# Experts without loops: two nested tests an expert, one test at the end for long lists, w_out four pieces ahead

## The chip, the cores and the metric

One core of one Trainium2 chip runs the whole kernel as one program. The metric is the device time of one execution in microseconds (us), and for the kernel before it is the median of three runs.

## The reference

Three stages follow each other, in fp32:

```
x   = attention(q_l, k_l, v_l, q_g, k_g, v_g)  # 4 x 8 heads, 512 local + 32 global tokens; local: window of 32 keys and the globals
e   = argmax(x @ w_gate)                       # x: 2176 tokens x 512; 8 experts, one per token
y   = gate_w * sigmoid(x @ w_output_gate)[e] * (relu(x @ w1[e]) @ w2[e])   # w1[e]: 512 x 1024, w2[e]: 1024 x 512
h   = y @ w_in;  g = (a0 + a1 h + a2 h^2 + a3 h^3) / (1 + |b0||h| + |b1| h^2 + 1e-6)
out = g @ w_out                                # w_in: 512 x 2048, w_out: 2048 x 512
```

The inputs give the eight experts 422, 331, 253, 249, 220, 149, 434 and 118 tokens. Which parts of the program run depends on these numbers, since the kernel tests them on the chip.

## The kernel before, in words

**Precision.** Every fp32 operand of the two MoE stages is split into a high and a low part (`hi`, `lo`, type fp32r), and each product is three matmuls: hi by hi, hi by lo, lo by hi. ScalarE (ACT) makes `hi` by a cast, and VectorE (DVE) or GpSimd (POOL) makes `lo` by a subtraction. The weights of an expert are 16 pieces of 128x512 in `slot[e % 2]`; while expert e computes, the pieces of expert e+1 are loaded into four `raw` buffers and split into the other slot (`split_set`, lines 697 to 701).

**Experts.** `wide(e)` (L884) computes the first 256 tokens of expert e (296 of expert 0): eight steps of 12 matmuls into `ph` (L898), a relu into `hT` (ACT L903, DVE L904), and, two steps later, 12 matmuls into `acc` (L910). At its end `acc` is copied to the tile `yt` (L916) and stored to `ybuf` (L839), and 512 entries of the expert's token list go from `idxT` to `toks` (L917); both stores are issued by ACT. A background generator (`todo`, L927) runs beside the matmuls by a plan: `s` splits a weight piece, `g` gathers a block of 128 tokens from `xbuf` (POOL, an indirect DMA into one of four `xg` buffers, L782), `x` scales it (ACT L794), `p` transposes it on TensorE (L807) and splits it (ACT L787, DVE L788). So the tokens of expert e+1 are prepared during expert e: three blocks, 384 tokens.

**Tokens beyond 256.** `single(e, j, x)` (L845) computes one block of 128 tokens. `beyond(e)` (L992) runs it behind a test on the chip, `cnt[e] > 256`; inside, a test `cnt[e] > 384` leads to `more` (L966), a loop of the hardware (`tc.For_i`, L968) over the blocks from the fourth on. An iteration transposes the block that was gathered before (L971), fetches the next one, runs `single` and stores 128 entries of the list column-wise to `toks` (L973). `beyond(e)` is called inside `wide(e + 1)`, behind its first step. For expert 0, one `single` behind a test (L1030) and a loop `more(0, j0, end0)` stand between `wide(0)` and `wide(1)`; with these inputs the loop has no iteration. Then block 2 of expert 1 is scaled and transposed (L1033, L1034), and `wide(1)` begins. With these inputs the test at L993 is true for experts 1 and 6, and the loop runs once, for expert 6.

**Conversion.** `w_in` and `w_out` come as 64-bit floats, and DVE makes fp32 of a piece by three integer operations (L718, L721, L724). `conv_step` (L735) does it for all 16 pieces of `w_in` and two of `w_out` (`NPRE = 2`) during experts 1 to 6, three pieces an expert, `c` in the plan. Two pieces `r64` are loaded ahead; the result stands in one tile `f32` (`NF = 1`) until SyncE's queue (SP) has stored it to `wf` in HBM (L742), from where it is loaded later like a weight.

**The second MoE stage.** `moe2` goes through 80 steps, five chunks of tokens by 16 columns of `w_in`. A step has 12 matmuls into `ph` (`gemm1`, L1111), the rational function on ACT, POOL and DVE (`elem`, L1114 to L1147), and matmuls of an earlier step into `acc` (`gemm2`, L1159). In the first 16 steps a generator `w_out` (L1179) brings one piece of `w_out` a step: a piece that was converted before is only split (L1193, L1194), any other is first converted on DVE by the same three operations. `columns` (L1213) turns the token list once, by a transpose into `acc3` and a copy by ACT to `order` (L1216), after step 2.

**What sets the order.** The order on every engine is the order in which the program issues: there is no planner. Engines wait for each other by semaphores. Before `moe2`, a test `off[7] < 512` (L1057) guards a reload of the first chunk, which expert 7's stage prepares ahead (`early`, L1041); it is false here.

Of the kernel before, what the change touches and what calls it, by code (L numbers as in the profile page):

```python
# [7 lines left out]
F32 = mybir.dt.float32  # L8
# [38 lines left out]
def plan(n, **at):  # L47

    o = [""] * n
    for t in "scxpg":  # L50
        for k in at.get(t, ()):
            o[k] += t
    return o


NPRE, NCONV = 2, 9

LOADS = [l for j in range(NPRE // 2) for l in ((4 * j, 4 * j + 2), (4 * j + 1,), (4 * j + 3,))]
# [13 lines left out]
STE = lambda nc, ch, i: nc.vector.tensor_copy if ch == 0 else nc.scalar.copy  # L72
LEAD = 2
WB = 1
NF = 1
YQ = lambda nc: nc.scalar
AQ = lambda nc: nc.gpsimd
AFTER = 1
# [25 lines left out]
class Build:  # L104
# [540 lines left out]
    def lists(self):  # L645

        self.nc.vector.tensor_tensor(out=self.wrap, in0=self.tab, in1=self.wrap, op=ALU.subtract)
        yield
        yield
        pt = self.ps_m.tile([128, 512], F32, tag="xps", name="lgT")[:, 0:128]  # L650
        self.nc.tensor.transpose(pt, self.wrap[:, 0:128], self.ident)
        yield
        self.nc.scalar.copy(self.idxT, pt)

    def ahead(self):

# [69 lines left out]

    def conv_init(self, pool):
        self.r64 = [pool.tile([128, 512], I64, name=f"r64_{n}") for n in range(2)]
        self.f32 = [pool.tile([128, 512], I32, name=f"f32_{n}") for n in range(NF)]

    def conv_first(self):
        for q in range(2):
# [2 lines left out]
    def conv_step(self, k):  # L735

        q, n = divmod(k, 3)
        if not 0 <= q < 16 + NPRE:
            return
        self.conv_op(self.r64[q % 2], self.f32[q % NF], n)  # L740
        if n == 2:
            CQ(self.nc).dma_start(out=self.wf[q], in_=self.f32[q % NF].bitcast(F32))  # L742
            if q + 2 < 16 + NPRE:
                n = q + 2 if q < 14 else 16 + 2 * (q - 14)
                CQ(self.nc).dma_start(out=self.r64[q % 2], in_=self.t["w64"][n])

    def counts(self):
# [15 lines left out]
        nc.vector.tensor_scalar(out=o[:, 2:3], in0=o[:, 2:3], scalar1=7, scalar2=None, op0=ALU.logical_shift_right)  # L763
        nc.vector.tensor_tensor(out=o[:, 2:3], in0=o[:, 2:3], in1=o[:, 3:4], op=ALU.mult)


    def expert_tiles(self, pool):
        mp, cp = self.mp, self.cp
        self.xs = pool.tile([128, 2, 4, FIRST], F32R, name="xs")
        self.xgs = [mp.tile([128, DM + 1], F32, name=f"xg{n}") for n in range(2)]  # L770
        for x in self.xgs:
            self.nc.gpsimd.memset(x, 0.0)
        ix = mp.tile([128, 5], I32, name="ix")
        self.idx0, self.ixo = ix[:, 0:3], ix[:, 3:5]
        self.cnt_i = cp.tile([1, 2, E], I32, name="cnt_i")
        self.cnt_f = cp.tile([1, 4, E], F32, name="cnt_f")
        c = cp.tile([1, 5], I32, name="cnt_x")
        self.cnt0, self.cnt_x = c[:, 0:1], c[:, 1:5]

    def gather(self, j, ix, n=NT, rows=128):  # L780

# [30 lines left out]
    def experts(self, st, first, gate):  # L812
# [29 lines left out]

            AQ(nc).dma_start(out=self.ybuf[:, :, FIRST:FIRST + 128], in_=y)

        def single(e, j, x, at=0, put=None):  # L845

            W = self.slot[e % 2]
# [36 lines left out]
        def wide(e, j, n, x, bg, last=True, acc=None, before=None):  # L884
# [29 lines left out]
            def end():  # L914
                for m in range(4):
                    (nc.scalar.copy, nc.vector.tensor_copy)[m % 2](yt[:, m, :n], acc[m][:, :n])  # L916
                YQ(nc).dma_start(out=self.toks[bass.ds(off[e], MOST), :].rearrange("(j p) o -> j (p o)", p=128),  # L917
                                 in_=self.idxT[NBLK * e:NBLK * e + MOST // 128])
                store(e, j, n, yt[:, :, :n], YQ(nc))

            if last:
# [36 lines left out]
        blocks = lambda e, bs=range(3): [(e, b) for b in bs if e < E]  # L958

        def fetch(e, i):  # L960

            ixo = self.ixo[:, 0:1]
            nc.gpsimd.tensor_copy(ixo, self.idx[:, bass.ds(i + NBLK * e, 1)])
            self.gather(NX - 1, ixo)

        def more(e, j, end):  # L966

# [18 lines left out]
        def expert(e, early=lambda: ()):  # L986

            plan = PLANW if e < E - 1 else PLANW7
            wide(e, 0, BASE, X(e), weave(todo(e, plan, None, blocks(e + 1), blocks(e, (3,)) + blocks(e + 1, (2,)) + blocks(e + 2, (0, 1))),
                                         iter(early())), before=(lambda: beyond(e - 1)) if e > 1 else None)  # L990

        def beyond(e):  # L992
            with tc.If(cnt[e] > BASE):  # L993
                single(e, 2, X(e), 256)
                with tc.If(cnt[e] > BASE + 128):
                    more(e, 3, (cnt[e] + 127) // 128)

        def woven():

            g, sp = self.gate(B - 1, woven=GW), todo(0, "s" * 8, 0)  # L1000
            for n in count():
                for _ in range(GS):
# [11 lines left out]
            yield from weave(todo(0, PLAN0, 1, blocks(1, (0, 1)) + blocks(0, (2, 3)),  # L1014
                                  blocks(1, (0, 1)) + blocks(0, (2, 3)) + blocks(2, (0, 1)) + blocks(1, (2,))),
                             self.lists())


# [2 lines left out]
        gate.close()  # L1021
        pools.append(PP("ps_t2", 1))
        self.conv_init(P("cv"))
        vals = nc.values_load_multi_w_load_instructions(self.cnt_i.rearrange("a b e -> a (b e)"), min_val=0, max_val=NT)[1]
        cnt, off[:] = vals[:E], vals[E:]
        more0, j0, end0 = nc.values_load_multi_w_load_instructions(self.cnt_x[:, 0:3], min_val=0, max_val=NBLK)[1]
# [14 lines left out]
        def early():  # L1041
            def steps():
                for _ in range(EL):
                    yield
                y0 = [x[:, :DM].rearrange("p (m t) -> p m t", m=4) for x in self.xgs[:3] + hr[:1]]
# [32 lines left out]
    def moe2(self):  # L1078
        nc, tc, out = self.nc, self.tc, self.t["out"]
        with ExitStack() as st:  # L1080
# [142 lines left out]
            for s in range(n + SK):  # L1223
# [104 lines left out]
```

## Time and profile before

| | us |
|---|---|
| median of three runs | 895.53 (894.07 to 903.0) |
| the profiled execution: time, span | 894.73, 892.8 |
| PE busy (share of the span) | 807.1 (90%) |
| DVE busy | 639.9 (72%) |
| ACT busy | 538.9 (60%) |
| POOL busy | 366.5 (41%) |

The page says where each engine is busy over the whole span. Three stretches have different limits: attention and routing up to about 190 us, the experts from there to 457 us, and `moe2` to the end. A busy share is an average over these, so the stretches are read one by one: the timeline (instructions in order of time, with the idle time of the engine before each and what ended it) and the table of windows (busy time of each engine in a stretch, with the granted TensorE clock).

### The profile page before, as it was taken

How to read it: one execution, taken by the hardware profiler on the slowest of the kernel's cores; microseconds unless marked ns; L12 is line 12 of the kernel's file. 1: busy time of each engine (PE TensorE's matmuls, PEld its weight loads, DVE VectorE, ACT ScalarE, POOL GpSimd, SP SyncE). 2: the span in 40 equal slices, each digit the busy share in tenths (PEclk: the TensorE clock that was granted, in tenths of full speed). 3: DMA queues.
4: the chain of work that ended last, by engine and by line, in shares of the span. 5: the costliest groups of instructions: out<-in, count | busy, mean ns of one | idle time of the engine just before them, and what ended most of it. 6: DMA issues, size and time to landing. Idle time of an engine off the chain costs nothing. (4 is left out here: it accounts for less than half of the span.)

```text
span 892.8 us, 17092 instructions
## 1 busy us (share of the span) xinstructions
PE 807.1 (90%) x6069; PEld 675.5 (76%) x6069; DVE 639.9 (72%) x1436; ACT 538.9 (60%) x1211; POOL 366.5 (41%) x409
## 2 busy tenths in 40 slices
PE   7999998986998999996778888789999999999994
PEld 4766765875988999974766666578887888988882
DVE  4778777752656887741349999997886888688684
ACT  3667666443554566631346655557777777778774
POOL 3445546452434666521434333443233323332422
PEclk9999999998998999998799999989999999999998
DMA  8798872581838799830431321200100000000000
GB/s 287 254 326 264 272 251 78 155 253 37 282 112 277 251 317 323 277 130 24 122 117 43 124 66 63 72 30 29 36 1 36 24 0 25 24 1 1 36 0 36
DMA packets 50512, 112.90 MB, mean 126 GB/s; under 512 B 9104, under 2 KB 22593, under 8 KB 48362
## 3 DMA queue, kind: packets, MB, share of 16 engines
q1 hardware_dynamic: 41642, 97.18, 34.1%
q0 software_dynamic: 4480, 10.14, 3.4%
q10 hardware_dynamic: 4288, 4.29, 1.4%
q8 instruction: 55, 0.90, 0.4%
q14 instruction: 47, 0.39, 0.1%
HBM read 96.99 MB, written 18.98 MB: 130 GB/s over the span
## 5 line engine op out<-in xcount | busy, mean ns | idle before, releaser
L1159 PE MATMUL acc<-slot,gh 128*128 128x512 f32 x544 | 174.6, 401 | 12.0 <-ACT gh L1132 3.3
L1123 POOL TENSOR_TENSOR q<-q,ab 128x384 f32<-128x384 f32 (+1 forms) x80 | 105.8, 1322 | 188.3 <-ACT q L1122 183.5
L1111 PE MATMUL ph<-x2c,slot 128*128 128x512 f32 (+1 forms) x576 | 136.1, 387 | 14.8 <-DVE u L1125 9.9
L701 POOL TENSOR_TENSOR slot<-raw,slot 128x512 fp32r<-128x512 f32 x80 | 109.0, 1366 | 94.8 <-ACT slot L697 89.5
L1111 PEld LDWEIGHTS ph<-x2c,slot 128*128 128x128 f32 x576 | 108.8, 194 | 38.0 <-DVE u L1125 13.0
L1159 PEld LDWEIGHTS acc<-slot,gh 128*128 128x128 f32 x544 | 102.3, 190 | 36.7 <-ACT gh L1132 4.6
L1159 PE MATMUL acc<-slot,gl 128*128 128x512 f32 x272 | 108.9, 400 | 0.5 <-DVE gl L1133 0.5
L910 PE MATMUL acc<-hT,slot 128*128 128x256 f32 (+1 forms) x768 | 104.9, 287 | 3.1 <-DVE hT L904 3.1
L910 PEld LDWEIGHTS acc<-hT,slot 128*128 128x128 f32 x768 | 97.9, 191 | 3.3 <-DVE hT L904 3.3
L697 ACT CAST slot<-raw 128x512 fp32r<-128x512 f32 x144 | 84.4, 618 | 14.1 <-DVE yt L916 5.2
L1132 ACT CAST gh<-u 128x384 fp32r<-128x384 f32 (+1 forms) x80 | 44.6, 557 | 77.2 <-DVE u L1147 76.4
L1140 DVE SCALAR_TENSOR_TENSOR q<-q,r 128x384 f32<-128x384 f32 (+1 forms) x80 | 50.0, 625 | 54.6 <-ACT r L1136 54.4
L1111 PE MATMUL ph<-xa,slot 128*128 128x384 f32 x384 | 74.6, 343 | 7.4 <-DVE u L1125 7.4
L1111 PEld LDWEIGHTS ph<-xa,slot 128*128 128x128 f32 x384 | 68.5, 191 | 13.2 <-DVE u L1125 11.0
L1135 ACT ACTIVATE r<-q,cab 128x384 f32<-128x384 f32 (+1 forms) x80 | 52.7, 659 | 42.3 <-POOL q L1123 42.3
L701 DVE TENSOR_TENSOR slot<-raw,slot 128x512 fp32r<-128x512 f32 x64 | 64.2, 1006 | 14.4 <-ACT slot L697 13.3
L317 POOL TENSOR_SCALAR pr<-ex,r 128x128 f32<-128x128 f32 x128 | 46.9, 379 | 65.2 <-PE sc L263 20.8
L898 PE MATMUL ph<-xa,slot 128*128 128x256 f32 x384 | 56.0, 302 | 12.1 <-issue 11.0
L898 PEld LDWEIGHTS ph<-xa,slot 128*128 128x128 f32 x384 | 52.7, 209 | 12.9 <-issue 11.2
L1159 PEld LDWEIGHTS acc<-slot,gl 128*128 128x128 f32 x272 | 51.7, 190 | 14.2 <-DVE gl L1133 2.1
L1122 ACT ACTIVATE q<-ab,cab 128x384 f32<-128x384 f32 (+1 forms) x80 | 59.8, 748 | 0.0
L299 ACT ACTIVATE ex<-sm,mx 128x128 f32<-128x128 f32 x128 | 50.3, 395 | 15.7 <-POOL pr L317 7.5
(207 smaller groups left out, 1529.5 us busy)
## 6 DMA issues: line engine op xcount, KB each, us to landing
raw<-in_w_dram SPq DMA_DIRECT2D x78, 512.0 KB
vw<-in_vw_dram SPq DMA_DIRECT2D x16, 1024.0 KB
r<-in_w_dram SPq DMA_DIRECT2D x18, 512.0 KB
kw<-in_kw_dram SPq DMA_DIRECT2D x16, 384.0 KB
wf<-f SPq DMA_DIRECT2D x18, 256.0 KB
raw<-wf SPq DMA_DIRECT2D x9, 512.0 KB
qt<-in_qT_dram SPq DMA_DIRECT2D x32, 128.0 KB
xbuf<-xrow SPq DMA_DIRECT2D x8, 512.0 KB
```

The lines of the kernel that those rows point to most:

```text
L299: nc.scalar.activation(ex[:, h], src[:, h], AF.Exp, bias=mx[:, h:h + 1], scale=-1.0, accum_out=ssum[:, h:h + 1])
L317: nc.gpsimd.tensor_scalar(out=pr[:, h], in0=ex[:, h], scalar1=r[:, h:h + 1], scalar2=1.0, op0=ALU.mult, op1=ALU.mult)
L697: nc.scalar.copy(hi, r)
L701: eng.tensor_tensor(out=lo[:, c], in0=r[:, c], in1=hi[:, c].bitcast(F32), op=ALU.subtract)
L898: nc.tensor.matmul(ph, lhsT=W[:, b, 2 * k + s // 4, c:c + 128], rhs=x[:, a, k, :n], start=(i == 0), stop=(i == 11))
L910: nc.tensor.matmul(acc[m][:, :n], lhsT=W[:, b, 8 + f, 128 * m:128 * m + 128], rhs=hT[f % nh][:, a, :n], start=(f == 0 and i == 0), stop=(f ...
L1111: nc.tensor.matmul(ph[:, :w], lhsT=l[a], rhs=r[b], start=(k == 0 and i == 0), stop=(k == 3 and i == 2))
L1122: nc.scalar.activation(q, ab, AF.Identity, scale=b1, bias=b0)
L1123: nc.gpsimd.tensor_tensor(out=q, in0=q, in1=ab, op=ALU.mult)
L1135: nc.scalar.activation(r0, q, AF.Ln, bias=eps1)
L1140: nc.vector.scalar_tensor_tensor(out=q, in0=q, scalar=1.0 + 1e-6, in1=r0, op0=ALU.add, op1=ALU.mult)
L1159: nc.tensor.matmul(accs[i], lhsT=l[a], rhs=Wo[:, b, f, :], start=(f == 0 and j == 0), stop=(f == 15 and j == 2))
```

## The change

1. `more` is no longer called for experts 1 to 7. The inner test leads to one more `single(e, 3, ...)`, whose block is prepared like the others: four blocks per expert are scaled and transposed during the expert before instead of three. The plans get one more `x` and `p` (and other places for `g`). Block 3 of expert 1 is gathered during expert 0 and scaled and transposed with block 2 between `wide(0)` and `wide(1)`.
2. Expert 0's loop stands behind a test (`again0 > 0`).
3. What lies beyond 512 tokens of any expert stands behind one test, `rare > 0`, at the end, where `off[7] < 512` stood. Behind it an expert's weights are loaded and split once more, and a loop runs over the rest of its list. `rare` is worked out with the other counts (three DVE operations) and loaded with them: five registers instead of three.
4. Each expert stores its whole list (up to 18 rows of 128) instead of four rows; the column-wise store of the loop is gone.
5. `NPRE = 4`: four pieces of `w_out` (0, 2, 4, 6) are converted ahead, the last two during expert 7. A second conversion buffer is taken from the tile `yt`, for the middle one of an expert's three pieces.
6. `columns` runs after step 1 instead of 2; the four blocks of the first chunk are loaded into the four `xg` buffers instead of three of them and `hr0`; the dead gather of expert 7's stage is gone.

```diff
-NPRE, NCONV = 2, 9
+NPRE, NCONV = 4, 9
-PLANW = plan(32, s=range(0, 31, 2), c=(2, 3, 4, 12, 13, 14, 22, 23, 24), g=(1, 6, 18, 24), x=(1, 2, 14), p=(5, 8, 19))
-PLANW7 = plan(32, s=range(2, 18, 2), g=(1,))
+PLANW = plan(32, s=range(0, 31, 2), c=(2, 3, 4, 12, 13, 14, 22, 23, 24), g=(1, 3, 18, 24), x=(1, 2, 14, 16), p=(5, 8, 19, 22))
+PLANW7 = plan(32, s=range(2, 18, 2), c=(4, 5, 6, 16, 17, 18))
-PLAN0 = plan(16, s=range(1, 9), g=(0, 0, 1, 2, 11, 12, 14), x=(6, 7, 9, 10), p=(7, 8, 11, 13))
+PLAN0 = plan(16, s=range(1, 9), g=(0, 0, 1, 2, 11, 12, 14, 15), x=(6, 7, 9, 10), p=(7, 8, 11, 13))
...
-        self.conv_op(self.r64[q % 2], self.f32[q % NF], n)
+        self.conv_op(self.r64[q % 2], self.f32[q % 3 % 2], n)
...
+        f = o[:, 4:5]
+        nc.vector.tensor_reduce(out=f, in_=self.cnt_i[:, 0], axis=AX.X, op=ALU.max)
+        nc.vector.tensor_scalar(out=f, in0=f, scalar1=MOST, scalar2=None, op0=ALU.is_gt)
+        nc.vector.scalar_tensor_tensor(out=f, in0=self.cnt_i[:, 1, E - 1:E], scalar=128 * CH[0], in1=f, op0=ALU.is_lt, op1=ALU.max)
...
                 with tc.If(cnt[e] > BASE + 128):
-                    more(e, 3, (cnt[e] + 127) // 128)
+                    single(e, 3, X(e), 384)
...
+        def reload(e):
+            w = yt.rearrange("p m t -> p (m t)")[:, 0:1024]
+            for pc in range(8):
+                ...
+                AQ(nc).dma_start(out=w, in_=src)
+                for q in range(2):
+                    hi, lo = (self.slot[1][:, i, 2 * pc + q, :] for i in range(2))
+                    nc.scalar.copy(hi, w[:, 512 * q:512 * q + 512])
+                    nc.vector.tensor_tensor(out=lo, in0=w[:, 512 * q:512 * q + 512], in1=hi.bitcast(F32), op=ALU.subtract)
+        def rest(e):
+            reload(e)
+            with tc.For_i(1, (cnt[e] + 127) // 128 - MOST // 128 + 1, 1) as k:
+                ...
+                single(e, None, self.xa, put=..., W=self.slot[1])
...
-        fetch(0, j0)
         with tc.If(more0 > 0):
             single(0, 2, self.xs, put=store_rest)
-        more(0, j0, end0)
-        self.scale(2, 128, S1)
-        self.prep(2, self.xa, ps_t(), 256, scale=False)
+        with tc.If(again0 > 0):
+            fetch(0, j0)
+            more(0, j0, end0)
+        for b in (2, 3):
+            self.scale(b, 128, S1)
+            self.prep(b, self.xa, ps_t(), 128 * b, scale=False)
...
         beyond(E - 1)
-        with tc.If(off[E - 1] < 128 * CH[0]):
+        with tc.If(rare > 0):
+            ...
+            for e in range(E):
+                with tc.If(cnt[e] > MOST):
+                    rest(e)
             for n in range(CH[0]):
-                self.load_y(n, nc.scalar)
+                self.load_y(n, AQ(nc))
                 self.x2_prep(n, self.x2c, n)
...
-                if s == 2:
+                if s == 1:
                     columns()
```

## Rows read from the trace of the kernel before

**Rows 1.** Timeline, expert 0's end: start, duration us, engine, line, [idle before <-releaser]

```profile
206.90 0.90 PE L880 MATMUL pt<-ident,hr 128*128 128x128 f32 x4 [0.52 <-ACT hr L876]
...
213.48 0.72 ACT L794 ACTIVATE xg<-xg 128x512 f32<-128x512 f32 x1 [5.00 <-issue]
...
214.26 1.11 PE L807 MATMUL pt<-ident,xg 128*128 128x128 f32 x4 [6.46 <-ACT xg L794]
...
215.02 6.09 PE L898 MATMUL ph<-xa,slot 128*128 128x256 f32 x36
215.41 0.59 ACT L787 CAST xa<-pt 128x512 fp32r<-128x512 f32 x1 [1.21 <-PE pt L807]
```

**Rows 2.** The loop's line L968: sequencer instructions, ns min/median/max, first to last start us

```profile
L968 ACTq EVENT_SEMAPHORE  x12: 38/38/2142, 210.0 to 213.2; - x12
...
L968 SPq EVENT_SEMAPHORE  x10: 27/28/562, 426.9 to 428.0; - x10
```

**Rows 3.** Timeline, expert 6's first single block, and the loop's last store

```profile
386.03 4.28 PE L865 MATMUL ph<-slot,x2c 128*128 128x512 f32 x18
...
398.69 0.90 PE L880 MATMUL pt<-ident,hr 128*128 128x128 f32 x4 [0.52 <-ACT hr L876]
...
419.43 0.57 POOL L973 DMA_DIRECT2D toks<-ix  x1
```

**Rows 4.** Timeline, wide(7) going on behind expert 6's loop

```profile
428.66 5.28 PE L898 MATMUL ph<-xa,slot 128*128 128x256 f32 x24 [10.99 <-issue]
...
433.77 1.58 PE L910 MATMUL acc<-hT,slot 128*128 128x256 f32 x12
```

**Rows 5.** Timeline, wide(2) going on behind expert 1's single block

```profile
256.48 3.00 PE L898 MATMUL ph<-x2c,slot 128*128 128x256 f32 x24 [0.78 <-ACTq L995]
```

**Rows 6.** Windows, wide(2) and wide(3): us, busy PE PEld DVE ACT POOL, PEclk, DMA, GB/s

```profile
256.50:286.60 30.10, 26.50 (x205) 25.99 (x205) 22.59 (x30) 15.79 (x32) 16.64 (x13) 0.89 0.67 226
286.60:311.70 25.10, 24.34 (x204) 24.14 (x204) 19.15 (x30) 15.62 (x32) 16.07 (x12) 1.00 0.80 256
```

**Rows 7.** Timeline, the end of wide(2)

```profile
272.61 0.33 SPq L742 DMA_DIRECT2D wf<-f  x1
...
277.68 2.18 DVE L718 TENSOR_SCALAR f<-r 128x512 int32<-128x512 int32 x1 [2.37 <-issue]
...
280.98 2.50 PE L910 MATMUL acc<-hT,slot 128*128 128x256 f32 x10 [3.09 <-DVE hT L904]
```

**Rows 8.** Timeline, a block's four transposes inside wide(4)

```profile
340.62 0.46 PEld L807 LDWEIGHTS pt<-ident,xg 128*128 128x128 f32 x4
```

**Rows 9.** Windows, steps 4 to 15 of moe2

```profile
489.40:580.00 90.60, 72.52 (x293) 55.36 (x292) 90.17 (x110) 51.91 (x85) 37.52 (x23) 0.96 0.27 82
```

**Rows 10.** Timeline of DVE, one operation of elem in three steps of moe2

```profile
481.34 0.68 DVE L1140 SCALAR_TENSOR_TENSOR q<-q,r 128x512 f32<-128x512 f32 x1
...
487.46 0.69 DVE L1140 SCALAR_TENSOR_TENSOR q<-q,r 128x512 f32<-128x512 f32 x1
...
495.05 0.69 DVE L1140 SCALAR_TENSOR_TENSOR q<-q,r 128x512 f32<-128x512 f32 x1
```

**Rows 11.** Timeline of PE, two following steps of moe2

```profile
489.41 2.96 PE L1111 MATMUL ph<-x2c,slot 128*128 128x512 f32 x12
...
495.01 2.96 PE L1111 MATMUL ph<-x2c,slot 128*128 128x512 f32 x12
```

**Rows 12.** The test before moe2: ACT's sequencer at L1057

```profile
L1057 ACTq COMPARE_BRANCH  x1: 58/58/58, 453.7 to 453.7; - x1
L1057 ACTq EVENT_SEMAPHORE  x1: 17/17/17, 457.2 to 457.2; - x1
```

**Rows 13.** Timeline, PE's first matmuls of moe2, and its wait for the order

```profile
457.24 13.01 PE L1111 MATMUL ph<-x2c,slot 128*128 128x512 f32 x48 [4.79 <-ACTq L1057]
...
481.60 1.22 PE L1159 MATMUL acc<-slot,gh 128*128 128x512 f32 x2 [3.18 <-ACT order L1216]
```

**Rows 14.** Timeline, the last operation of the counts

```profile
177.30 0.15 DVE L764 TENSOR_TENSOR cnt_x<-cnt_x 1x1 int32<-1x1 int32 x1
```

More of the change, by code (lines that the diff above doesn't have):

```diff
@@ L74 @@
 WB = 1
-NF = 1
 YQ = lambda nc: nc.scalar
@@ L649, in lists @@
         yield
-        pt = self.ps_m.tile([128, 512], F32, tag="xps", name="lgT")[:, 0:128]
-        self.nc.tensor.transpose(pt, self.wrap[:, 0:128], self.ident)
+        pt = self.ps_m.tile([128, 512], F32, tag="xps", name="lgT")
+        self.nc.tensor.transpose(pt[:, 0:128], self.wrap[:, 0:128], self.ident)
         yield
-        self.nc.scalar.copy(self.idxT, pt)
+        self.nc.scalar.copy(self.idxT, pt[:, 0:128])
     def ahead(self):
@@ L728, in conv_init @@
         self.r64 = [pool.tile([128, 512], I64, name=f"r64_{n}") for n in range(2)]
-        self.f32 = [pool.tile([128, 512], I32, name=f"f32_{n}") for n in range(NF)]
+        self.f32 = [pool.tile([128, 512], I32, name="f32")]
     def conv_first(self):
@@ L739, in conv_step @@
             return
-        self.conv_op(self.r64[q % 2], self.f32[q % NF], n)
+        self.conv_op(self.r64[q % 2], self.f32[q % 3 % 2], n)
         if n == 2:
-            CQ(self.nc).dma_start(out=self.wf[q], in_=self.f32[q % NF].bitcast(F32))
+            CQ(self.nc).dma_start(out=self.wf[q], in_=self.f32[q % 3 % 2].bitcast(F32))
             if q + 2 < 16 + NPRE:
@@ L776, in expert_tiles @@
         self.cnt_f = cp.tile([1, 4, E], F32, name="cnt_f")
-        c = cp.tile([1, 5], I32, name="cnt_x")
-        self.cnt0, self.cnt_x = c[:, 0:1], c[:, 1:5]
+        c = cp.tile([1, 6], I32, name="cnt_x")
+        self.cnt0, self.cnt_x = c[:, 0:1], c[:, 1:6]
     def gather(self, j, ix, n=NT, rows=128):
@@ L843, in store_rest, with single @@
             AQ(nc).dma_start(out=self.ybuf[:, :, FIRST:FIRST + 128], in_=y)
-        def single(e, j, x, at=0, put=None):
-            W = self.slot[e % 2]
+        def single(e, j, x, at=0, put=None, W=None):
+            W = W or self.slot[e % 2]
             hk = lambda a, k: hT[AFTER + k // 2][:, a, 128 * (k % 2):128 * (k % 2) + 128]
@@ L916, in end @@
                     (nc.scalar.copy, nc.vector.tensor_copy)[m % 2](yt[:, m, :n], acc[m][:, :n])
-                YQ(nc).dma_start(out=self.toks[bass.ds(off[e], MOST), :].rearrange("(j p) o -> j (p o)", p=128),
-                                 in_=self.idxT[NBLK * e:NBLK * e + MOST // 128])
+                k = min(NBLK, 128 - NBLK * e)
+                YQ(nc).dma_start(out=self.toks[bass.ds(off[e], 128 * k), :].rearrange("(j p) o -> j (p o)", p=128),
+                                 in_=self.idxT[NBLK * e:NBLK * e + k])
                 store(e, j, n, yt[:, :, :n], YQ(nc))
@@ L956, in todo @@
                 yield
-        blocks = lambda e, bs=range(3): [(e, b) for b in bs if e < E]
+        blocks = lambda e, bs=range(4): [(e, b) for b in bs if e < E]
         def fetch(e, i):
@@ L964, in fetch @@
             self.gather(NX - 1, ixo)
+        spare = yt.rearrange("p m t -> p (m t)").bitcast(I32)[:, 0:512]
         def more(e, j, end):
@@ L988, in expert @@
             plan = PLANW if e < E - 1 else PLANW7
-            wide(e, 0, BASE, X(e), weave(todo(e, plan, None, blocks(e + 1), blocks(e, (3,)) + blocks(e + 1, (2,)) + blocks(e + 2, (0, 1))),
+            wide(e, 0, BASE, X(e), weave(todo(e, plan, None, blocks(e + 1), blocks(e + 1, (2, 3)) + blocks(e + 2, (0, 1))),
                                          iter(early())), before=(lambda: beyond(e - 1)) if e > 1 else None)
@@ L995, in beyond @@
                 with tc.If(cnt[e] > BASE + 128):
-                    more(e, 3, (cnt[e] + 127) // 128)
+                    single(e, 3, X(e), 384)
+        def reload(e):
+            w = yt.rearrange("p m t -> p (m t)")[:, 0:1024]
+            for pc in range(8):
+                src = (self.t["w1"][e][:, pc, :] if pc < 4 else self.t["w2"][e][:, 2 * pc - 8:2 * pc - 6, :].rearrange("p a f -> p (a f)"))
+                AQ(nc).dma_start(out=w, in_=src)
[6 more added lines that the diff above has]
+            with tc.For_i(1, (cnt[e] + 127) // 128 - MOST // 128 + 1, 1) as k:
+                r0 = nc.s_assert_within(off[e] + cnt[e] - 128 * k, 0, NT)
+                ix, tok = self.ixo[:, 0:1], self.ixo[:, 1:2].bitcast(F32)
+                AQ(nc).dma_start(out=tok, in_=self.toks[bass.ds(r0, 128), :])
+                nc.gpsimd.tensor_copy(ix, tok)
+                self.gather(NX - 1, ix)
+                self.prep(NX - 1, self.xa, ps_t(), 0)
+                single(e, None, self.xa, put=lambda y: AQ(nc).dma_start(out=self.ybuf[:, :, bass.ds(r0, 128)], in_=y),
+                       W=self.slot[1])
         def woven():
@@ L1014, in woven @@
             yield from weave(todo(0, PLAN0, 1, blocks(1, (0, 1)) + blocks(0, (2, 3)),
-                                  blocks(1, (0, 1)) + blocks(0, (2, 3)) + blocks(2, (0, 1)) + blocks(1, (2,))),
+                                  blocks(1, (0, 1)) + blocks(0, (2, 3)) + blocks(2, (0, 1)) + blocks(1, (2, 3))),
                              self.lists())
@@ L1044, in steps @@
                     yield
-                y0 = [x[:, :DM].rearrange("p (m t) -> p m t", m=4) for x in self.xgs[:3] + hr[:1]]
+                y0 = [x[:, :DM].rearrange("p (m t) -> p m t", m=4) for x in self.xgs]
                 for n, y in enumerate(y0):
```

8 lines of the change are left out of this document (7 added, 1 removed).

## The prediction

> **What bounds the kernel now.** I read the timeline of TensorE (PE) first, for its idle stretches, then the same stretches on the other engines, and then the windows, to see which engine fills a stage.
>
> Between experts PE is held up by control flow. Behind expert 0's block it ends its transposes at 207.80 (206.90 + 0.90) and goes on at 214.26, after 6.46 us [rows 1]. Expert 0's loop has no iteration, yet its line holds ACT's sequencer with semaphore instructions from 210.0 to 213.2, one of them for 2.14 us [rows 2]: all engines meet there, and nothing else runs. Behind expert 6's loop PE is idle for 10.99 us [rows 4]; the meeting there starts at 426.9 [rows 2], 6.9 us after the loop's column-wise store had been issued (419.43 + 0.57) [rows 3]. A test without a loop behind it is cheap: behind expert 1's block PE goes on after 0.78 us [rows 5].
>
> Inside the wide stages PE is the bound: in wide(3) it is busy for 24.34 of 25.10 us [rows 6]. Wide(2) takes 30.10 us. Near its end DVE's first conversion operation waits for 2.37 us and takes another 2.18, the relu behind it comes late, and PE waits for 3.09 us [rows 7]; the clock then falls, and the stage has a mean granted share of 0.89 against 1.00 [rows 6]. What the conversion waited for fits the single buffer: the store that empties it was issued at 272.61 [rows 7].
>
> In the first 16 steps of moe2 DVE is the bound, busy for 90.17 of 90.60 us [rows 9], and PE waits for it. From step 16 on nothing is changed.
>
> **The parts of the change, costed.** The sum stands against the profiled execution, 894.73 us; the median of the runs shown is 0.80 above it.
>
> *A, expert 0's end.* The empty loop goes, a false test takes its place, and a second block is scaled and transposed before wide(1). I price the test by the nearest row, 0.78 us from PE's last transpose to the next work [rows 5], so ACT scales at 208.6. One round is 0.72 for the scale, 0.06 to the transposes (213.48 + 0.72 to 214.26), 1.15 from there to the cast (to 215.41) and 0.59 for it [rows 1]: 2.52. The second scale stands behind the first cast on ACT, and the second transposes behind that scale, at 211.9; wide(1) starts 0.76 behind them (215.02 - 214.26), at 212.6 instead of 215.02 [rows 1]. Gain 2.4. Bounds: 4.0 if PE's clock doesn't fall this time, since its first 36 matmuls took 6.09 us [rows 1] and 24 at the high clock 3.00 [rows 5], so 36 would take 4.5; and -1.0 if the false test costs ACT the 3.4 us that it costs at the end (453.7 to 457.2) [rows 12]. The gather of block 3 takes the place of the removed fetch on POOL, one for one.
>
> *B, expert 6's blocks.* From the end of the first block (398.69 + 0.90 = 399.59) [rows 3] to the end of wide(7)'s 24 matmuls, at 433.77 [rows 4], there are 34.2 us. After: a second block as long as the first, 399.59 - 386.03 = 13.56 [rows 3], then the exit, 0.78, and the 24 matmuls at the high clock, 3.00 [rows 5]: 17.3. Gain 16.8. Its transposes are in E. Bounds: 17.6 without any exit gap, 13.4 if one jump is missed at 3.4 [rows 12].
>
> What is late next there is the load of the first chunk's `ybuf` blocks on SP, which waits for this block's store, with splits on ACT, and relus behind them. Its cover is the steps of wide(7) before the first split. Without the loop this store is the last one: that is a rival below.
>
> *C, the conversion buffer.* The middle piece goes to `yt`, so the third piece's operations no longer wait for the middle piece's store. Gain: wide(2) falls to wide(3)'s length, 30.10 - 25.10 = 5.0 [rows 6]. Bounds 0, if something else made DVE wait, and 5.0. The new waits, of `yt`'s copy at a stage's end for the store of the middle piece and of the middle piece for `yt`'s own store, each have about half a stage between them, 12 us; I take nothing.
>
> *D, two pieces of w_out.* In moe2 a step of DVE with a piece's three conversion operations takes 7.59 us (487.46 to 495.05), one without them 6.12 (481.34 to 487.46) [rows 10]. Two pieces less: gain 2.9. Bounds: 0, if the freed time turns into waits, and 4.0, where PE with 5.60 a step (489.41 to 495.01) [rows 11] becomes the bound. The conversions move into expert 7's stage, where nothing follows them closely; their stores and loads pass SP there, and I take nothing.
>
> *E, the fourth block.* In wide(1) to wide(6), one more block each: 0.46 us of PE's weight loads [rows 8], on PE and so on the path: -2.8. Bounds: 0, since wide(3) has 0.76 us of PE idle [rows 6], and -7.9 if ACT's share, 0.72 + 0.59 a block [rows 1], were on the path.
>
> *F, the test before moe2.* PE waits there for 4.79 us [rows 13], for ACT, whose branch at 453.7 is followed by its next instruction at 457.2 [rows 12]. The body now spans eight experts' code on all engines. ACT's jump already pays this price over a short body, and the others would pay it at the same time, so I take 0, with 3.4 us either way.
>
> By the Trainium skill ("Runtime: NRT & Kernel Launch", section "Instruction fetch mechanics") a taken branch whose target lies outside two prefetched pages stalls on a fetch of the target page; that speaks against the longer body and the new test. ACT's 3.4 us agrees with it; the 0.78 us behind expert 1's block shows a jump that it spares.
>
> *G, the rest.* Three operations more in the counts, at 0.15 us [rows 14], delay the list that PE transposes next: -0.5 with the two registers more; bounds 0 and -1. `columns` a step earlier takes away a wait of PE of 3.18 us [rows 13], but DVE fills this stretch, so 0 (at best 3.2). The longer list stores are one DMA each as before and nobody waits for them before moe2: 0.
>
> Sum: 2.4 + 16.8 + 5.0 + 2.9 - 2.8 - 0.5 = 23.8, so 870.9 for the profiled execution, and 871.7 with the 0.80 up to the median.
>
> **The rivals.**
> *R1, the jumps miss.* ACT at expert 0's new test and one engine at the long body each lose 3.4 us [rows 12]: 871.7 + 6.8 = 878.5. For it: a jump does cost that once, and every jump target moves with the code. Against it: the exit behind expert 1's block [rows 5]. This is the rule named above, at work twice. Chance 0.17.
> *R2, wide(2)'s stall stays or moves*, because the loads of weights in the same queue, and not the one buffer, made DVE late, or because the store in expert 6's tail holds up wide(7) through the loads of `ybuf`, for about as long: 871.7 + 5.0 = 876.7. For it: the meeting at 426.9 shows some store landing about 7 us after the last issue [rows 2, 3]. Against it: that store was column-wise and is gone. Chance 0.15.
> *R3, slower: DVE becomes the bound of the wide stages.* DVE has 19.15 busy of 25.10 us in wide(3), and in wide(2) one late DVE operation cost 5.0 [rows 6]. Should the fourth block's split push a relu late in this way in each of wide(1) to wide(6), that is 30.0, and 901.7. It takes 23.8 / 6 = 4.0 us a stage to eat the gain. Against it: one subtraction more a stage, on an engine with 6 us free in wide(3). Chance 0.04.
> *R4, the cost of a loop only moves*: what the loop's end collected, the stores and the semaphores, is collected at the next test, and B gives 2 instead of 16.8: 886.5, or 891.5 with wide(2)'s stall. Chance 0.04.
> That the change isn't exercised can be left out: the loop runs once for expert 6, so its tokens fit the fourth block, and the long lists' test is false for all.
>
> **The numbers.** My forecast has 0.60: 871.7. Independent misses of a few us each (A 3.4, C 5.0, D 2.9, E 5.1, F 3.4) partly cancel; the range from 863 to 882 takes in R1 and R2 and leaves out R3 and R4. A difference of 1% (9 us) is about what a measurement of this kernel can tell from no change. Forecast, R1 and R2 are faster by more: 0.92. R4 is at that bound: 0.04 for no change. R3: 0.04.
>
> **What would show it.** No line of a loop in the trace of experts; PE idle under 1 us between expert 6's two blocks and behind them, and wide(7)'s first matmuls at the high clock; wide(2) near 25.5 us, with DVE's first conversion operation never waiting for a store; wide stages some 0.5 us longer; steps of moe2 at 6.1 us for two more pieces; PE's idle time before moe2 near 4.8 us. Wrong would be: PE waiting for DVE's relu in several wide stages (R3), a new wait of over 3 us at a test (R1), ACT waiting for a `ybuf` block in wide(7) (R2), or a gap of 10 us that has only another name (R4).

## The result and the profile after

The changed kernel takes 872.87 us (median of 4 runs, 869.64 to 875.25) against 898.66 for the kernel before beside it: a ratio of 0.971, with an interval of 0.964 to 0.978. The profiled execution took 869.64 us, its span is 867.7 against 892.8. Its busy times, from the page:

```profile
span 867.7 us, 17050 instructions
PE 800.7 (92%) x6093; PEld 670.5 (77%) x6093; DVE 640.9 (74%) x1445; ACT 545.4 (63%) x1223; POOL 364.0 (42%) x403
```

The lines that answer to expert 0's end [rows 1], from the timeline (start, duration, engine, line, idle time before and its releaser):

```profile
208.08 0.90 PE L884 MATMUL pt<-ident,hr 128*128 128x128 f32 x4 [0.52 <-ACT hr L880]
...
209.81 0.72 ACT L798 ACTIVATE xg<-xg 128x512 f32<-128x512 f32 x1 [0.16 <-ACTq L1064]
210.58 0.66 PE L811 MATMUL pt<-ident,xg 128*128 128x128 f32 x4 [1.61 <-ACT xg L798]
...
211.76 0.72 ACT L798 ACTIVATE xg<-xg 128x512 f32<-128x512 f32 x1
212.54 1.11 PE L811 MATMUL pt<-ident,xg 128*128 128x128 f32 x4 [1.30 <-ACT xg L798]
213.30 6.83 PE L902 MATMUL ph<-xa,slot 128*128 128x256 f32 x36
```

PE idles for 1.61 and 1.30 us where it idled for 6.46, and `wide(1)` starts 5.22 us behind the start of the block's last transposes (208.08) instead of 8.12. Its first 36 matmuls now take 6.83 us instead of 6.09. The granted clock is as low as before over the same stretch, here in the windows of before and then of after; `wide(1)` only begins earlier in it:

```profile
211.60:218.50 6.90, 4.24 (x20) 4.25 (x21) 0.81 (x2) 2.98 (x6) 1.75 (x2) 0.51 0.00 1
```

```profile
211.60:218.50 6.90, 5.96 (x28) 5.97 (x29) 3.11 (x6) 4.12 (x8) 3.17 (x3) 0.51 0.07 24
```

(us, busy PE, PEld, DVE, ACT, POOL, then the granted clock, the DMA share, GB/s; PEld is the weight load of PE.)

Expert 6's tail, which answers to [rows 3, 4]:

```profile
381.88 4.28 PE L869 MATMUL ph<-slot,x2c 128*128 128x512 f32 x18
394.54 0.90 PE L884 MATMUL pt<-ident,hr 128*128 128x128 f32 x4 [0.52 <-ACT hr L880]
395.19 4.37 PE L869 MATMUL ph<-slot,x2c 128*128 128x512 f32 x18
407.93 0.90 PE L884 MATMUL pt<-ident,hr 128*128 128x128 f32 x4 [0.52 <-ACT hr L880]
408.62 3.13 PE L902 MATMUL ph<-xa,slot 128*128 128x256 f32 x24
...
435.01 13.87 PE L1154 MATMUL ph<-x2c,slot 128*128 128x512 f32 x48 [4.75 <-ACTq L1092]
```

The second block and `wide(7)` carry no idle time ahead of them at all. From the first block's start to the end of the 24 matmuls there are 29.87 us by these rows (408.62 + 3.13 - 381.88) instead of 47.91 (433.94 - 386.03).

The windows of `wide(2)` to `wide(5)`, which answer to [rows 6] (columns as above):

```profile
255.93:280.94 25.01, 24.41 (x208) 24.20 (x208) 21.14 (x30) 16.77 (x34) 16.87 (x13) 1.00 0.69 230
280.94:306.36 25.42, 24.74 (x209) 24.55 (x209) 19.47 (x32) 16.58 (x34) 16.20 (x12) 1.00 0.91 303
306.36:331.44 25.08, 24.47 (x209) 24.26 (x209) 19.99 (x32) 16.88 (x34) 15.93 (x12) 1.00 0.89 298
331.44:357.47 26.03, 24.90 (x208) 24.61 (x209) 19.65 (x32) 16.87 (x34) 15.92 (x12) 1.00 0.92 305
```

`wide(2)` has lost its stall and its lower clock; PE is the bound in all four.

**Where the time went.** I cut both traces at the same instructions (matmuls, and in `moe2` one activation of ACT a step):

```
stretch                                         before    after     gain
program's start to expert 0's single block      193.37   194.57     -1.2
block's start to wide(1)                         21.65    18.73      2.9
wide(1)                                          41.46    42.62     -1.2
wide(2)                                          30.08    25.01      5.1
wide(3) to expert 6's first single block         99.47   100.94     -1.5
expert 6's blocks and 24 matmuls of wide(7)      47.74    29.71     18.0
the rest of wide(7) and the test                 23.47    23.42      0.0
moe2 up to step 0                                 8.21     9.07     -0.9
steps 0 to 15                                   120.29   117.36      2.9
steps 16 to 79                                  293.30   292.84      0.5
```

The sixth row ends at the next matmul's start, so it is 0.1 to 0.2 shorter than by the lines above. These add to 24.6 of the 25.1 us between the spans. In `moe2 up to step 0` the granted clock is 0.71 against 0.79 before.

### The profile page after: what moved, and what is told of

It reads as the page before. It is cut to its first block, busy times and chain, and to the rows that moved or that the text cites. A ratio compares the mean times of both kernels' runs of the same rounds, so it can differ in the third digit from the quotient of the medians.

```text
span 867.7 us, 17050 instructions
## 1 busy us (share of the span) xinstructions
PE 800.7 (92%) x6093; PEld 670.5 (77%) x6093; DVE 640.9 (74%) x1445; ACT 545.4 (63%) x1223; POOL 364.0 (42%) x403
## 5 line engine op out<-in xcount | busy, mean ns | idle before, releaser
L914 PE MATMUL acc<-hT,slot 128*128 128x256 f32 (+1 forms) x768 | 103.1, 284 | 0.0
L1154 PEld LDWEIGHTS ph<-xa,slot 128*128 128x128 f32 x384 | 68.7, 191 | 13.2 <-DVE u L1168 11.0
L700 DVE TENSOR_TENSOR slot<-raw,slot 128x512 fp32r<-128x512 f32 x64 | 61.5, 965 | 15.8 <-ACT slot L696 14.7
L1190 DVE SCALAR_TENSOR_TENSOR u<-u,cab,r 128x384 f32<-128x384 f32 (+1 forms) x80 | 59.9, 749 | 2.4
L1164 ACT ACTIVATE u<-ph,cab 128x384 f32<-128x384 f32 (+1 forms) x80 | 56.7, 708 | 0.1
```

The lines of the kernel that those rows point to most:

```text
L700: eng.tensor_tensor(out=lo[:, c], in0=r[:, c], in1=hi[:, c].bitcast(F32), op=ALU.subtract)
L914: nc.tensor.matmul(acc[m][:, :n], lhsT=W[:, b, 8 + f, 128 * m:128 * m + 128], rhs=hT[f % nh][:, a, :n], start=(f == 0 and i == 0), stop=(f ...
L1154: nc.tensor.matmul(ph[:, :w], lhsT=l[a], rhs=r[b], start=(k == 0 and i == 0), stop=(k == 3 and i == 2))
L1164: nc.scalar.activation(u, h, AF.Identity, scale=a3, bias=a2)
L1190: nc.vector.scalar_tensor_tensor(out=u, in0=u, scalar=a0, in1=r0, op0=ALU.add, op1=ALU.mult)
```

## The experiments

The start of expert 0's first single block, ahead of everything that was changed, scatters from 193.37 (before) to 203.85 (`one_buffer`) over the fourteen traces. So spans of single executions are not compared here; stages are, and "the rest" is the span less that start: 699.4 before, 673.1 after, and 671.9 in `after_again`, the changed kernel run once more (872.22 us, ratio 0.973, 0.967 to 0.978):

> The changed kernel once more, beside the one with SP's stores. Theory: the same stage lengths as in its first trace within 0.3 us, while the attention stage ahead differs by several us from run to run.

Its stages repeat those of after within some 0.3 us (`wide(2)` 24.99, steps 0 to 15 117.30), with two exceptions where the lower clock falls otherwise: `wide(1)` takes 41.87 instead of 42.62, its first 36 matmuls 6.07 instead of 6.83, and `moe2` up to step 0 8.70 instead of 9.07.

**`blocks_only`: the kernel before with the fourth block alone (no loop for experts 1 to 7).**

```diff
-PLANW = plan(32, ..., g=(1, 6, 18, 24), x=(1, 2, 14), p=(5, 8, 19))
+PLANW = plan(32, ..., g=(1, 3, 18, 24), x=(1, 2, 14, 16), p=(5, 8, 19, 22))
-        blocks = lambda e, bs=range(3): ...
+        blocks = lambda e, bs=range(4): ...
-            ... blocks(e, (3,)) + blocks(e + 1, (2,)) + blocks(e + 2, (0, 1))),
+            ... blocks(e + 1, (2, 3)) + blocks(e + 2, (0, 1))),
-                    more(e, 3, (cnt[e] + 127) // 128)
+                    single(e, 3, X(e), 384)
```

> The kernel before with one part of the change: four blocks an expert prepared ahead, and expert 6's loop replaced by a second single block behind the nested test. Expert 0's empty loop, the one conversion buffer, the two pieces ahead and the short test at the end stay. Theory (the loop's end costs, and a test doesn't): from expert 6's first single block to the end of wide(7)'s next 24 matmuls 29.7 us instead of 47.7, so 18.0 gained, less six transposed blocks at 0.46 (2.8): 15.2 us under the kernel before, ratio 0.983. Rival (the cost of the loop's end is collected at the next test): PE idle some 10 us behind the second block, gain 2 to 4 us, ratio 0.996. Wide(2) keeps its 30 us, as the buffer is the old one.

Measured: 878.21 us, ratio 0.976 (0.970 to 0.981). Its PE timeline around expert 6's blocks:

```profile
395.29 4.28 PE L865 MATMUL ph<-slot,x2c 128*128 128x512 f32 x18
...
408.60 4.39 PE L865 MATMUL ph<-slot,x2c 128*128 128x512 f32 x18
421.37 0.90 PE L880 MATMUL pt<-ident,hr 128*128 128x128 f32 x4 [0.52 <-ACT hr L876]
422.06 3.13 PE L898 MATMUL ph<-xa,slot 128*128 128x256 f32 x24
```

It is the picture of after: this part alone takes the loop's whole cost away, 26.77 us from the first block to `wide(7)` (26.74 in after), and R4 falls. Up to the end of `wide(7)`'s 24 matmuls it gains the 18.0 that I expected. The ratio of 0.983 that I expected lies outside the interval; by "the rest", 684.3, this trace gains 15.1. Its wide stages with one conversion buffer are long:

```profile
258.66:287.41 28.75, 25.60 (x208) 25.10 (x208) 22.46 (x31) 16.87 (x34) 16.09 (x13) 0.95 0.67 216
287.41:314.58 27.17, 26.50 (x209) 26.30 (x209) 18.68 (x31) 16.87 (x34) 16.17 (x12) 0.93 0.82 265
...
341.85:370.98 29.13, 26.55 (x209) 26.14 (x209) 20.63 (x32) 16.87 (x34) 15.89 (x12) 0.94 0.82 268
```

`wide(2)` to `wide(5)` sum to 112.3 us, against 105.6 before and 101.5 after. How much of that the fourth block makes is not shown: `one_buffer`, next, has four blocks and one buffer too, and takes 106.6.

**`one_buffer`: after with the middle piece in the first buffer again.**

```diff
-        self.conv_op(self.r64[q % 2], self.f32[q % 3 % 2], n)
+        self.conv_op(self.r64[q % 2], self.f32[0], n)
```

(and the same in the store behind it)

> The changed kernel with one conversion buffer for all pieces, as before. Theory (the third piece's operations wait for the store of the middle piece): wide(2), 25.0 us in the changed kernel, goes back to about 30, with a DVE wait of 2 to 4 us before its third piece and PE waiting some 3 us for a relu; span + 5.0 us, about 873 against 867.7. Rival (traffic of the weight loads made DVE late, and the change moved it): wide(2) stays at 25.0, span unchanged.

Measured: `wide(2)` takes 27.95 us and `wide(5)` 28.10, the four stages 106.6 against 101.5. The timeline at the end of `wide(2)`:

```profile
279.69 0.33 SPq L741 DMA_DIRECT2D wf<-f  x1
...
284.35 1.47 DVE L717 TENSOR_SCALAR f<-r 128x512 int32<-128x512 int32 x1 [1.04 <-DMA wf<-f]
...
288.95 1.45 PE L914 MATMUL acc<-hT,slot 128*128 128x256 f32 x10 [2.65 <-DVE hT L908]
```

This is the chain of [rows 7], and here the profile names the releaser: DVE waits for the store that empties the buffer, the relu behind it is late, PE waits. In after the same operation starts without a wait, and the store ahead of it leaves from `yt`:

```profile
271.12 0.33 SPq L741 DMA_DIRECT2D wf<-yt  x1
...
274.66 0.41 DVE L717 TENSOR_SCALAR f<-r 128x512 int32<-128x512 int32 x1
```

In size it was less than before's 5.0: PE waits for 2.65 us instead of 3.09, and the clock, 0.89 in the mean of before's `wide(2)` [rows 6], stays at 1.00 here. In `wide(5)` the wait has another form. DVE waits for the store for 0.31 us alone, but the last conversion operation of the third piece takes 2.51 us (0.68 in `wide(2)` of before), so DVE copies the output late, ACT stores it late and comes late to the test, and PE waits there:

```profile
365.76 2.51 DVE L723 SCALAR_TENSOR_TENSOR f<-r,f 128x512 int32<-128x512 int32 x1
...
371.12 1.09 PE L902 MATMUL ph<-x2c,slot 128*128 128x256 f32 x7 [2.41 <-ACTq L1000]
```

With one buffer it is never the same: before has a stall in `wide(2)` alone; `no_column_store` (below), the same code up to expert 6's loop, has the second form, 2.35 and 2.36 us at the test, in `wide(3)` and `wide(5)`, 27.17 and 27.31, and none in `wide(2)`, 24.58; `blocks_only` has the first form in `wide(2)`, the second in `wide(4)` and `wide(5)`, and in `wide(3)` the lower clock alone (0.93, no such wait). What holds up the slow operation was not tested; POOL works beside it each time. In every trace of the two-buffer kernel without further work, `wide(2)` is 24.7 to 25.0 us.

**`two_ahead`: after with `NPRE = 2`.**

```diff
-NPRE, NCONV = 4, 9
+NPRE, NCONV = 2, 9
-PLANW7 = plan(32, s=range(2, 18, 2), c=(4, 5, 6, 16, 17, 18))
+PLANW7 = plan(32, s=range(2, 18, 2))
```

> The changed kernel with two pieces of w_out converted ahead instead of four. Theory (DVE sets the first 16 steps of moe2, a piece without conversion saves 1.47 us): from step 0 to step 16 120.3 us instead of 117.4, span + 2.9; expert 7's stage unchanged. Rival (PE or a load sets them): under 1 us.

Measured: steps 0 to 15 take 120.28 us instead of 117.36: 2.92. Where a piece is converted ahead, DVE's step is 6.19 us, from the timeline of DVE in after:

```profile
473.69 0.68 DVE L1183 SCALAR_TENSOR_TENSOR q<-q,r 128x512 f32<-128x512 f32 x1
...
479.88 0.69 DVE L1183 SCALAR_TENSOR_TENSOR q<-q,r 128x512 f32<-128x512 f32 x1
```

**`no_column_store`: before without the loop's store of the list (rows 3's last line; the list's copy in memory then lacks expert 6's last block).**

```diff
                 single(e, i, X(e))
-                AQ(nc).dma_start(out=self.toks[bass.ds(off[e] + 128 * i, 128), :], in_=tok, ...)
```

> The kernel before without the column-wise store of 128 list entries at the end of the loop's body; this leaves expert 6's last block out of the token order. Theory (the meeting at the loop's end waits for the landing of that store): only the block's own store is left, which expert 0's loop waited for until 2.6 us after its issue; the meeting behind expert 6's loop ends near 422 us instead of 427.5, and PE is idle there for some 5.5 us instead of 11.0. Rival (the wait is for code behind the jump, or for the block's store): 10 to 11 us as before.

Measured: PE's idle time behind the loop is 5.35 us instead of 10.99 [rows 4].

```profile
426.44 3.83 PE L898 MATMUL ph<-xa,slot 128*128 128x256 f32 x17 [5.35 <-issue]
```

So half of that gap was this store, for which the meeting of the engines waited; the other half stays with the loop's end.

**`no_test` and `short_body`: after without the last test, and with only the reload of the first chunk behind it.**

```diff
         beyond(E - 1)
-        with tc.If(rare > 0):
-            ...
```

> The changed kernel without the test for long lists and without its body; experts over 512 tokens, which these inputs don't have, would not be computed. Theory (ACT's jump over the body costs 3.4 us, and PE waits for it): PE's idle time before moe2 falls from 4.75 to about 1.3 us (a test without a miss behind expert 7), and the clock stays high: 4 to 5 us under the changed kernel. Rival (the wait is the end of expert 7's stage, ACT's stores and casts): 4 us or more of idle time stay.

```diff
         with tc.If(rare > 0):
-            ...
-            for e in range(E):
-                with tc.If(cnt[e] > MOST):
-                    rest(e)
             for n in range(CH[0]):
```

> The changed kernel with the test for long lists, but behind it only the reload of the first chunk, as before; experts over 512 tokens are left out. Theory (ACT misses the jump over a short body and over a long one, for the same price): PE idle before moe2 4.75 us, as with the long body. Rival (a short body's end is within what has been fetched, and the kernel before had bad luck in its place): 1.3 us. Second rival (a long body costs more): under 4.75.

Measured: PE waits for 1.27 us without the test, for 1.51 with the short body, for 4.75 with the long one. Sequencers of ACT and of PE's weight load at the test, with the short body and then in after (ns min/median/max, first to last start):

```profile
L1092 ACTq COMPARE_BRANCH  x1: 50/50/50, 434.0 to 434.0; - x1
L1092 ACTq EVENT_SEMAPHORE  x1: 17/17/17, 434.2 to 434.2; - x1
L1092 PEldq COMPARE_BRANCH  x1: 222/222/222, 433.0 to 433.0; - x1
```

```profile
L1092 ACTq COMPARE_BRANCH  x1: 50/50/50, 431.5 to 431.5; - x1
L1092 ACTq EVENT_SEMAPHORE  x1: 17/17/17, 434.9 to 434.9; - x1
L1092 PEldq COMPARE_BRANCH  x1: 3392/3392/3392, 430.5 to 430.5; - x1
```

ACT's jump takes 0.2 us over the short body and 3.4 over the long one. It is not alone: over the long body PE's own jump takes 3.39 us and ends at 433.9, 1.0 ahead of ACT's, and DVE's takes 3.0 (430.9 to 433.9). In before ACT alone was late: PE's took 0.25, DVE's 0.2. My expectation that the body's length would not matter, since before's short body [rows 12] cost 3.4, fell. In the traces with a short body the jump cost that in before and in `no_column_store` (PE waits 4.79 and 4.77) and not in `short_body` and `blocks_only` (1.51 and 1.50); with the long body PE waited for 4.5 to 4.9 in all nine traces, and its own jump took 3.4 to 4.4. The clock follows: just behind the test it is at the lower of its two levels in after and not with the short body (windows, columns as above):

```profile
433.50:440.30 6.80, 5.29 (x12) 4.13 (x13) 4.04 (x3) 3.22 (x6) 4.52 (x3) 0.50 0.23 73
```

```profile
434.27:440.00 5.73, 5.73 (x25) 4.65 (x26) 4.48 (x3) 5.09 (x9) 4.96 (x4) 1.00 0.53 181
```

From the last matmul of `wide(7)` to step 0 there are 9.0 us in the two traces where the short body's jump was quick (`short_body`, `blocks_only`), 13.3 in before, and 13.1 to 14.1 with the long body: it costs 3.2 us of waiting (4.75 - 1.51) and 4.1 to 5.1 in all, with the clock.

**`fourth_of_6`: after, with the fourth block scaled and transposed ahead for experts 1 and 6 alone** (the others' aren't used with these inputs).

```diff
-            wide(e, 0, BASE, X(e), weave(todo(e, plan, None, blocks(e + 1), ...
+            wide(e, 0, BASE, X(e), weave(todo(e, plan, None, blocks(e + 1, range(4 if e == 5 else 3)), ...
```

> The changed kernel with the fourth block scaled, transposed and split for experts 1 and 6 alone (the other lists are shorter than 385). Theory (a block costs PE's transposes, 0.46 us, and nothing else): wide(1) to wide(4) and wide(6) each 0.4 to 0.5 us shorter, span - 2.3. Rival (ACT's 1.31 us a block are on the path): 1.3 each, 6.5 in all.

Measured: 24.71, 24.96, 24.70 and 23.96 us for `wide(2)`, `wide(3)`, `wide(4)` and `wide(6)`, which is 0.30, 0.46, 0.38 and 0.45 less than in after: 0.40 a block, near the transposes' 0.46 [rows 8] and far from the rival's 1.31. But `wide(5)`, which still prepares four blocks here (those of expert 6), is 0.58 shorter too (25.45 against 26.03; an idle time of PE of 0.46 is gone), so a difference of this size also comes without a block less.

**`fifth_prep` and `fifth_sp`: after with block 3 transposed and split twice, and the same with an expert's two stores, of `ybuf` and of its list, issued by SP instead of ACT.** They look for R3.

```diff
-PLANW = plan(32, ..., p=(5, 8, 19, 22))
+PLANW = plan(32, ..., p=(5, 8, 19, 22, 25))
-  ... todo(e, plan, None, blocks(e + 1), ...
+  ... todo(e, plan, None, blocks(e + 1) + blocks(e + 1, (3,)), ...
```

> The changed kernel with block 3 of every expert transposed and split a second time: the fourth block's cost doubled. Theory (PE is the bound, DVE and ACT have room): wide(1) to wide(6) 0.46 us longer each, span + 2.8. Rival R3 (DVE or ACT come to the bound and make relus late): stalls of PE of over 1 us in several stages, span + 8 or more.

Measured: the four stages take 27.05, 27.39, 27.13 and 27.40, each about 2.0 us more than in after (1.4 in `wide(5)`), and not the 0.46 that I expected. Timeline at the end of `wide(2)`:

```profile
278.33 1.29 POOL L786 DMA_INDIRECT xg<-xbuf,idx  x1
...
279.25 2.25 DVE L700 TENSOR_TENSOR slot<-raw,slot 128x512 fp32r<-128x512 f32 x1
279.64 1.30 POOL L700 TENSOR_TENSOR slot<-raw,slot 128x512 fp32r<-128x512 f32 x1
...
281.43 0.74 DVE L920 COPY yt<-acc 128x256 f32<-128x256 f32 x2
282.31 0.38 ACTq L843 DMA_DIRECT2D ybuf<-yt  x1
282.73 0.62 ACT L696 CAST slot<-raw 128x512 fp32r<-128x512 f32 x1 [2.58 <-DVE yt L920]
...
283.73 1.46 PE L902 MATMUL ph<-xa,slot 128*128 128x256 f32 x10 [2.20 <-ACTq L1000]
```

DVE is not the bound in its sum; it is late at one place. Its subtraction takes 2.25 us beside POOL's gather and subtraction, where it takes 0.69 alone, and ends 0.56 behind the latter; so the copies of the output come late, ACT holds at the store of `ybuf` that waits for them, and comes late to the test behind it, for which PE waits 2.20 us. By the Trainium skill ("SBUF — State Buffer", section "SBUF: two separate sides") a DVE operation with two inputs in SBUF and a POOL operation that reads SBUF exclude each other for a whole instruction, the one that starts first going first. The rows agree in the end of DVE's, and don't show which came first: DVE's starts 0.39 us ahead of POOL's subtraction and is the one held up.

> The kernel with the fifth transposed block an expert, whose stages were 2.0 us longer each and whose PE waited 2.2 us at each false test, with an expert's two stores issued by SP instead of ACT. Theory (DVE's copy of yt is late behind a subtraction that POOL holds up; ACT waits for it to issue the store, comes late to the test, and PE waits for ACT): without the store ACT comes early, PE's wait at the tests falls from 2.2 to 0.6 us or less, and wide(2) is 25.5 us or less instead of 27.05. Rival (the longer wait is for code behind the jump): 2.2 and 27.0 stay.

Measured: the four stages take 25.34, 25.70, 25.45 and 25.71, the waits at the tests are 0.52 to 0.54.

```profile
280.09 2.18 PE L902 MATMUL ph<-xa,slot 128*128 128x256 f32 x16 [0.52 <-ACTq L1000]
```

So it was ACT's wait to issue these stores, and not DVE's sum, that cost 2 us a stage.

**`columns_later`: after with `columns` behind step 2 again.**

```diff
-                if s == 1:
+                if s == 2:
                     columns()
```

> The changed kernel with the token order transposed after step 2 of moe2, as before. Theory (DVE sets these steps, so PE's wait for the order costs nothing): PE waits again for ACT's copy of the order, some 3 us, and from step 0 to step 16 it is 117.4 us as in the changed kernel, within 0.3. Rival (PE's wait was on the path and the earlier transpose gained it): 119 to 120.5 us.

Measured: PE waits for the order once more, and the steps 0 to 15 take 117.32 us (117.36 in after). PE's timeline:

```profile
459.48 1.13 PE L1202 MATMUL acc<-slot,gh 128*128 128x512 f32 x2 [3.18 <-ACT order L1259]
```

**`sp_stores`: after, with both stores of an expert on SP and both scales of expert 0's end ahead of the transposes.**

```diff
-YQ = lambda nc: nc.scalar
+YQ = lambda nc: nc.sync
...
             self.scale(b, 128, S1)
+        for b in (2, 3):
             self.prep(b, self.xa, ps_t(), 128 * b, scale=False)
```

> The changed kernel with the experts' stores issued by SP instead of ACT, and with both scales of expert 1's blocks 2 and 3 ahead of both transposes. Theory: PE's 1.30 us between the two transposes goes, so wide(1) starts 17.4 us after the first single block's start instead of 18.7; ACT comes to each test about 1 us earlier, which takes up to 0.6 us from each of the waits behind wide(2) to wide(5) and about 1 us from the one before moe2; 3 to 5 us under the changed kernel, and a ratio near 0.967 to the kernel before. Rival (SP waits for yt with the weight loads behind it): casts late in the wide stages, no gain.

Measured: 870.68 us, ratio 0.969 (0.963 to 0.974); `after_again` beside it has 872.22. In the trace the places are there: PE's second wait at expert 0's end is 0.88 instead of 1.30, `wide(1)` starts 17.42 us behind the block's start instead of 18.73 and 19.04, the wide stages are 0.1 to 0.3 shorter.

```profile
218.08 0.66 PE L811 MATMUL pt<-ident,xg 128*128 128x128 f32 x4 [0.88 <-ACT xg L798]
```

The rest is 670.1, 1.8 to 3.1 less than in the two traces of the changed kernel. That is less than I expected. The gain of 1 us before `moe2` did not come: PE waits there for 4.56 us. ACT is through its jump at 436.7, but PE's own lasts until 438.3 (sequencers at the test):

```profile
L1093 ACTq EVENT_SEMAPHORE  x1: 17/17/17, 436.7 to 436.7; - x1
L1093 PEldq COMPARE_BRANCH  x1: 4052/4052/4052, 434.2 to 434.2; - x1
```

The timed difference of 1.5 us lies inside both intervals: a version that is no worse, not one that is shown to be better.

## Why the prediction was right

It gave 871.7 us and a range from 863 to 882; measured were 872.87 and 872.22. The forecast's own case came about. Of its four gains B, C and D have a run of their own; A is read from the traces alone. By its steps:

- **A, 2.4.** The start of `wide(1)` gained 2.9 (2.6 in `after_again`), and 2.2 to the end of its first 36 matmuls, which took 0.74 longer. Over the traces it lies 21.7 to 22.0 us behind the block's start with the loop and 18.1 to 19.4 without (17.4 in `sp_stores`). The case that the clock stays up (4.0) failed: from 211.6 to 218.5 the granted clock was 0.51, as in before. The 36 matmuls took longer as `wide(1)` began earlier in that stretch (28 of PE's matmuls in its window against 20, transposes included). Where it falls differs from trace to trace: they took 5.55 to 6.09 in the three traces with the loop and 5.54 to 6.83 in the eleven without. The new test cost ACT no missed jump.
- **B, 16.8.** Measured 18.0. The term that was mis-sized is the exit: I took 0.78 behind the second block, from expert 1's [rows 5], and there is none, so the 24 matmuls end 2.8 us behind the block's transposes instead of 3.8; the second block adds 13.4 instead of 13.56. `blocks_only` shows the same with this part alone, and `no_column_store` shows what the gap of 10.99 was.
- **C, 5.0.** Measured 5.1, with the fourth block inside it. `one_buffer` brings the wait back, and names its releaser. What I had not seen is that with one buffer this stall comes by chance in place, size and form: 5.1 us over the four stages in `one_buffer`, of which 2.9 in `wide(2)` come as forecast and 2.1 in `wide(5)` through ACT's late store and the test. That the whole 5.0 stood in `wide(2)` of before, its lower clock included, is luck of that trace. R2 did not come about: in after neither `wide(2)` nor `wide(7)` has such a wait of PE.
- **D, 2.9.** Measured 2.93, and 2.92 by `two_ahead`.
- **E, -2.8.** Four stages lost 1.5 us net (`wide(3)` to `wide(6)`), 0.25 to 0.50 each, and by `fourth_of_6` a block costs about 0.40, which makes 2.4 for six. The term stands, within what that run can tell.
- **F, 0.** Right in its number, by luck. PE's gap is 4.75 against 4.79. That the other engines would pay at the same time as ACT is what after shows (PE 3.39, DVE 3.0). But that a short body costs ACT the same is not so: before's happened to miss its jump, and two other kernels with a short body don't. Had before not missed it, the term would have been -3.2 in the wait and -4.1 to -5.1 in all. By the Trainium skill ("Runtime: NRT & Kernel Launch", section "Instruction fetch mechanics") a jump beyond the prefetched pages stalls; the long body that missed in all nine traces agrees with it, and that a short one misses in one kernel and not in another fits a matter of where its code lies, which no run here shows directly.
- **G, -0.5.** Of the 1.2 us by which expert 0's block starts later, 0.8 are lost from the counts on: 0.43 in the counts, for whose list PE waits (2.03 us against 0.17), and 0.42 just ahead of the block, where PE idles for 0.66 us instead of 0.24. So it is in every trace of the changed kernel and its variants (2.6 to 2.7 us from the counts' start to the list's transpose against 2.2, and 0.65 to 0.72 against 0.19 to 0.24). That `columns` a step earlier is worth 0 is shown by `columns_later`: PE loses 3.18 and the stretch nothing, as DVE sets its length.

The errors (B +1.2, G -0.3, 0.9 lost at `moe2`'s start, where the clock was lower) partly cancel. R1 did not come about at the new test, and R4 is refuted by `blocks_only`. R3 did not come about in the changed kernel, but it was near: one more prepared block a stage makes 7.4 us over four stages (`fifth_prep`), through ACT's store ahead of a test and not through a relu.

## What to carry to other kernels

A hardware loop in a chain of experts is paid by its end, and here by a store still under way when it ended; a test around straight code cost PE 0.6 to 0.8 us in after, where its jumps were quick. Price a jump at both values, and on every engine, since which one a kernel gets can change from kernel to kernel over the same lines. And where an engine stands idle in sum, look at what is queued behind the one late operation: in `fifth_prep` one DMA issue ahead of a test turned one more prepared block into 2 us a stage.

## What the runs showed of the hardware

- ACT's jump over a short body took 3.4 us in before [rows 12] and in `no_column_store`, and 0.2 in `short_body` and `blocks_only`. PE's own jump took 0.2 over the short body in all four, and 3.4 to 4.4 over the long body in nine traces.
- At expert 0's end the granted clock from 211.6 to 218.5 was 0.51 in before, where PE had idled for 6.46 us, and in after, where it had idled for 1.61 and 1.30.
- A subtraction of DVE took 2.25 us beside POOL's gather and subtraction and 0.69 alone (`fifth_prep`).
- The stages ahead of expert 0's single block, almost the same code in all traces, ended over a spread of 10.5 us (193.37 to 203.85); the three latest, 200.3 and more, have stretches of the lower clock shortly ahead of it, but so has `columns_later`, 194.54. `wide(2)` to `wide(4)` repeat within 0.1 us in the two traces of the changed kernel.
